# A fused retention and phase-MLP kernel: order of the DMA queue, two more transposes by DMA, and the place of the z products

## The chip, the cores and the metric

The kernel runs on one core of a Trainium2 chip. The core has TensorE (PE) for matrix products, VectorE (DVE), ScalarE (ACT) and GpSimd (POOL) for elementwise work, and SyncE (SP), which here only issues transfers to the core's 16 DMA engines. Every engine executes its own instructions in the order in which they were written, and waits at its head for what the next instruction needs; so does SyncE's queue. The metric is the device time in microseconds (us).

## The reference

The first half is a linear recurrence (retention) for 4 batches and 8 heads of 64 channels over 768 tokens; the second is an MLP that mixes tokens and channels (512 of them), with a sine and a cosine of a projection.

```python
state = gamma * state + einsum('bhd,bhe->bhde', k[:, :, t], v[:, :, t])     # per head
y[:, :, t] = scale * einsum('bhd,bhde->bhe', q[:, :, t], state)
x = y.transpose(0, 2, 1, 3).reshape(B, S, H * D)
theta = x @ w_theta
zr, zi = x * cos(theta), x * sin(theta)
u = x + w_tok_r @ zr + w_tok_i @ zi                                          # over tokens
out = u + max(u @ w_ch, 0)
```

Inputs and outputs are float32; the kernel works in bfloat16 and sums in float32.

## The kernel before

**The work and its tiles.** A *pair* is 256 tokens of one batch (all heads); there are 3 pairs per batch and 12 in all, numbered n = 0 to 11, and batch b is pairs 3b to 3b+2. An *output tile* is 128 tokens by 512 channels; there are 6 per batch and 24 in all, numbered m. Names below such as x(5) or u(5) mean the x tile of pair 5 and the u tile of output tile 5.

**Retention of a pair.** `load` (L76) brings k, q and v in float32 from DRAM, 512 KB each, into a pool of 7 buffers. `prep` (L161) casts them to bfloat16 with the decay factors (k on ScalarE, q and v on GpSimd in the later slots), in tiles named kqb. k and q are needed transposed: `flip` (L179) does that with 8 TensorE transposes into PSUM (tag "tr") and a VectorE copy out; `flip_dma` (L193) does it with one DMA transpose issued by SyncE, from SBUF to SBUF. Before the change, k goes by DMA from pair 7 on (`K_DMA`), q from pair 10 on (`Q_DMA`, L63). `ret_A` makes a block of scores (two blocks per pair, one PSUM buffer), `ret_mask` (L213) masks it on VectorE, `ret_Y` and `ret_I` make the output, transposed, from the scores and from the state, `ret_S` updates the state. `ret_out` copies the output to xT on ScalarE.

**The second half.** xT is turned into x by TensorE (`x_pe`) for pairs 0 to 4 and by a DMA transpose (`x_dma`, L288) from pair 5 on (`X_DMA`). `theta` (L309) projects xT on TensorE, and ScalarE takes the cosine and sine. `zmul` (L319) multiplies them by x on VectorE: two instructions per pair, which wait for x. `moe_M` (L327) sums the 12 products of an output tile over the batch's 6 time blocks, into one PSUM buffer (tag "y", one buffer, for most tiles). `moe_u` (L344) adds x on VectorE and so frees that buffer. `moe_U` (TensorE) or `moe_U_dma` (DMA, from slot 9 on) transposes u, `moe_O` (L365) makes the last product and `moe_out` (L372) the output tile, ot, on VectorE. `store` (L378) writes it to DRAM.

**The order.** It is written out by hand (the pools only wait for buffers). After a prologue for pairs 0 to 2, the main loop (L582) has slots n = 3 to 12. Slot n finishes pair n-1, starts pair n, prepares pair n+1, loads pair n+3, sums the output tiles `mine` (one tile in slots 3 to 6, two in slots 7 to 12), and finishes the tiles `done` of the slot before. A batch's tiles can be summed only when the z of its three pairs are there: tiles 6 and 7, of batch 1, are summed in slot 7, from z(3), z(4) and z(5), and z(5) is made in slot 6. After the loop the last tiles follow one by one.

In SyncE's queue, slot 6 holds: kT of pair 7, load of k of pair 9, x(5), loads of q and v of pair 9, the store of tile 3. In slot 7 and 8 the order is the same, one pair later; from slot 9 on there are no loads, and the transposes of u stand between. [...]

On VectorE, slots 5 and 6 (`early_z`, L670) have the two z products ahead of u of the slot's tile, slot 4 one of them; slots 7 to 12 have them after u of the first tile, ahead of u of the second and of the outputs (in slot 12 after u of its first tile, ahead of the outputs).

Of the kernel before, what the change touches and what calls it, by code (L numbers as in the profile page):

```python
# [14 lines left out]
FT = mybir.dt.float32  # L15
BF = mybir.dt.bfloat16
# [5 lines left out]
def _bcast_last(ap: bass.AP, n: int) -> bass.AP:  # L22
    return bass.AP(tensor=ap.tensor, offset=ap.offset, ap=list(ap.ap) + [[0, n]])


def _bcast_mid(ap: bass.AP, n: int) -> bass.AP:
    pat = list(ap.ap)
    return bass.AP(tensor=ap.tensor, offset=ap.offset,
                   ap=[pat[0], [0, n]] + pat[1:])
# [3 lines left out]
def kernel(  # L33
# [18 lines left out]
    B, H, S, D = q.shape  # L52
    dm = H * D
    P = 128
    HP = P // 2
    nT = S // P
# [3 lines left out]
    gammas = [1.0 - 2.0 ** (-5.0 - h) for h in range(H)]  # L60
    nG = nT // 2

    K_DMA, Q_DMA, X_DMA, U_DMA = 2 * nG + 1, 3 * nG + 1, 2 * nG - 1, 3 * nG  # L63

    ctx.enter_context(tc.manual_schedule())

# [2 lines left out]
    work = ctx.enter_context(tc.tile_pool(name="work", bufs=3))  # L69
# [6 lines left out]
    def load(n, name):  # L76

        b, g = divmod(n, nG)
        t = io.tile([P, H, 2 * D], FT, name="pair", bufs=7)
        src = dict(k=k, q=q, v=v)[name]  # L80
        nc.sync.dma_start(out=t, in_=src[b, :, 2 * g * P:2 * (g + 1) * P, :].rearrange(  # L81
            "h (p two) d -> p h (two d)", two=2))
        raw[n, name] = t
# [66 lines left out]
    for i in range(2):  # L150
        t = const.tile([P, NP, P], BF, name=f"stbd{i}")
# [9 lines left out]

    def prep(n, name, engines):
        g = n % nG
        t = work.tile([P, 2, dm], BF, name="kqb", bufs=10)
        src = raw[n, name].rearrange("p h (two d) -> p two h d", two=2)
        dst = t.rearrange("p two (h d) -> p two h d", h=H)
        if name == "k":
            if engines[0] is nc.scalar:
                nc.scalar.copy(dst, src)
            else:  # L170
                engines[0].tensor_copy(dst, src)
        else:
            sc = qscp if name == "q" else vscp
            for two in range(2):
                engines[two].tensor_mul(dst[:, two], src[:, two],  # L175
                                        _bcast_last(sc[:, 2 * g + two], D))
        st[n, name] = t
# [15 lines left out]
    def flip_dma(n, name):  # L193
        t = work.tile([P, 2, NP, P], BF, name="kqT", bufs=6)
        nc.sync.dma_start_transpose(out=t.rearrange("p w j t -> p (w j) t"),
                                    in_=st[n, name].rearrange("p w d -> p (w d)"))
        st[n, name + "T"] = t
# [40 lines left out]
    def ret_I(n, a):  # L238

        c = 2 * (n % nG) + a  # L240
        half = slice(a * HP, (a + 1) * HP)
        yT = st[n, "y"][a]
        if c > 0:
            for j in range(NP):
                nc.tensor.matmul(yT[:, j, :], stbd[c % 2][:, j, :],  # L245
                                 st[n, "qT"][:, :, j, half], start=False,
                                 stop=False, skip_group_check=True)
# [40 lines left out]
    def x_dma(n):  # L288
        b, g = divmod(n, nG)
        nc.sync.dma_start_transpose(  # L290
            out=xs[b][:, 2 * g:2 * g + 2, :].rearrange("p a (j e) -> p (a j) e", j=NP),
            in_=st[n, "xT"].rearrange("p a j t -> p (a j t)"))
# [26 lines left out]
    def zmul(n, a):  # L319
        b, g = divmod(n, nG)  # L320
        c = 2 * g + a
        nc.vector.tensor_mul(zs[b][:, c], st[n, "cs", a], _bcast_mid(xs[b][:, c, :], 2))  # L322
# [27 lines left out]
    def moe_U_dma(m):  # L350
        uT = work.tile([P, nD, P], BF, name="uT", bufs=4)
        nc.sync.dma_start_transpose(out=uT, in_=mo[m]["u"])
        mo[m]["uT"] = uT
# [17 lines left out]

    def moe_out(m):  # L372
        b, t0 = divmod(m, nT)
        ot = work.tile([P, dm], FT, name="ot", bufs=4)
        nc.vector.scalar_tensor_tensor(ot, mo[m]["o"], 0.0, mo[m]["u"], ALU.max, ALU.add)  # L375
        mo[m]["ot"] = ot

    def store(m):  # L378
        b, t0 = divmod(m, nT)
        nc.sync.dma_start(out=out[b, t0 * P:(t0 + 1) * P, :], in_=mo[m]["ot"])  # L380
# [3 lines left out]
    def w_cast(t0):  # L384
        for r in range(2):
            row = work.tile([P, S], BF, name="wrow", bufs=5)
            nc.gpsimd.tensor_copy(row, wdma[r, t0])
            wrow[r, t0] = row
# [79 lines left out]
    DP, PP = (DV, PL), (PL, PL)  # L468
# [106 lines left out]
    tiles_of = {nG - 2: [], nG - 1: [0, 1]}  # L575
    for m in range(2, nT):
        tiles_of[nG + m - 2] = [m]
    for n in range(nG + 4, B * nG + 1):
        m = nT + 2 * (n - nG - 4)
        tiles_of[n] = [m, m + 1]  # L580
    pairs = range(B * nG)
    for n in range(nG, B * nG + 1):  # L582
        mine, done = tiles_of[n], tiles_of[n - 1]
        late, two = n > nG, len(mine) > 1
        nxt = n + 1 in pairs

        if nxt and n + 1 >= K_DMA:
            flip_dma(n + 1, "k")
        if n + 3 in pairs:
            load(n + 3, "k")  # L590
        if n >= U_DMA:
            moe_U_dma(done[1])
        def preps(engines):
            prep(n + 1, "q", engines)
            prep(n + 1, "v", PP)
            if n in (nG, nG + 1):
                w_cast(n - nG + 4)

        if n == nG:
            nc.gpsimd.tensor_copy(wch, wdma["ch"])  # L600
        if nxt and n > nG + 2:
            preps(PP)
        if late:
            ret_I(n - 1, 1)

        if n in pairs:
            ret_A(n, 0)
            ret_mask(n, 0)
        if n == nG:
            moe_M(0, 5, nT)  # L610
            w_flip(1, 2)
            moe_u(0)
            moe_M(1, 4, nT)
            moe_u(1)
        if late:
            ret_Y(n - 1, 1)
            ret_S(n - 1, 1)
            ret_out(n - 1, 0, nc.scalar.copy)
            ret_out(n - 1, 1, nc.scalar.copy)
            state_out(n - 1, 1)  # L620
            if n < nG + 3:
                prep(n + 1, "k", (PL,))
                if n > nG + 1:
                    preps(DP)
            if n - 1 >= X_DMA:
                x_dma(n - 1)
        if n + 3 in pairs:
            load(n + 3, "q")

        first = mine[0]  # L630
        moe_M(first, 0, 3 if two else 2)
        if late:
            theta(n - 1, 0)
            if n - 1 < X_DMA:
                x_pe(n - 1)
            if n == nG + 1:
                preps(DP)
            theta(n - 1, 1)
        if two:
            moe_M(first, 3, nT)  # L640
            moe_u(first)
        for name, limit in (("k", K_DMA), ("q", Q_DMA)):
            if nxt and nG + 1 < n + 1 < limit and (n > nG + 1 or name == "k"):
                flip(n + 1, name)
        if n + 1 >= K_DMA and not two:
            moe_M(first, 2, 4)
        if nxt and n + 1 >= Q_DMA:
            flip_dma(n + 1, "q")
        if n + 3 in pairs:
            load(n + 3, "v")  # L650
        for t in tiles_of[n - 2]:
            store(t)
        if n + 1 >= U_DMA:
            moe_U_dma(first)

        if n in pairs:
            ret_S(n, 0)
            state_out(n, 0)
            ret_A(n, 1)
            ret_mask(n, 1)  # L660
            ret_Y(n, 0)
            ret_I(n, 0)
        if n < U_DMA:
            moe_U(done)
        if n == nG:
            prep(n + 1, "k", (AC,))
            preps(DP)
        if n == nG or n + 1 < K_DMA and not two:
            moe_M(first, 2, 4)
        early_z = late and not two  # L670
        if early_z and n > nG + 1:
            zmul(n - 1, 0)
        if n < nG + 3:
            w_tok(n - nG + 3)
        if early_z:
            zmul(n - 1, 0 if n == nG + 1 else 1)
        if not two:
            moe_M(first, 4, nT)
            if n == nG + 1:
                flip(n + 1, "q")  # L680
            moe_u(first)
            if n == nG + 1:
                zmul(n - 1, 1)
        elif n in pairs:
            moe_M(mine[1], 0, nT)
        if n + 2 in pairs and n > nG + 1:
            prep(n + 2, "k", (AC,))
        if late and not early_z:
            zmul(n - 1, 0)
            zmul(n - 1, 1)  # L690
        if two and n in pairs:
            moe_u(mine[1])
        for i, t in enumerate(done):
            if n == nG:
                flip(n + 1, "kq"[i])
            moe_O(t)
            moe_out(t)
        if n not in pairs:
            moe_M(mine[1], 0, nT)
            moe_u(mine[1])  # L700
# [43 lines left out]
```

## Time and profile before

| | |
|---|---|
| median of 14 runs | 172.72 us (169.3 to 175.29) |
| the profiled execution | 174.05 us, its span 172.3 us |
| TensorE, VectorE, ScalarE, GpSimd busy | 157.0, 102.9, 79.0, 65.3 us |
| DMA | 37.92 MB, mean 220 GB/s |
| matrix products over tokens (L340), TensorE | 97.9 us |
| DMA transposes of k or q, of x, of u | 7, 7 and 15; 4.2, 3.2 and 2.7 us from issue to landing (median) |
| loads of k, q, v of a pair | 7.1, 7.6 and 8.1 us from issue to landing (median) |

In the lines that follow, a wait is written as "engine line waited for: total us, times, longest us". In the chain and the timelines the columns are the start in us from the start of the span, the duration in us, and what ran. "SPq" is SyncE's queue, and its durations are those of the issue, not of the transfer. In the row PEclk each digit is the granted TensorE clock in one of 40 equal slices of the span, in tenths of full speed. Busy times are given with their share of the span.

### The profile page before, as it was taken

The page shows a single profiled execution, that of the slowest core. Times are in us where ns is not written, and L with a number is a line of the kernel's source. Part 1 is how long each engine was busy: PE and PEld are TensorE (multiplying, and loading weights), DVE is VectorE, ACT ScalarE, POOL GpSimd, SP SyncE. Part 2 cuts the span into 40 slices and gives each one's busy share as a digit, 9 for nine tenths or more (in the row PEclk, how much of TensorE's full clock was granted, in tenths as well). Part 3 has the DMA queues.
Part 4 walks back from the last instruction along what each step waited for, and adds up shares of the span by engine and source line. Part 5 has one row for each costly group of instructions (what it writes and reads, how often), then busy time and mean ns, then how long its engine had stood idle before and what let it go on. Part 6 is the DMA issues. An engine that isn't in the chain of part 4 may idle for free.

```text
span 172.3 us, 4660 instructions
## 1 busy us (share of the span) xinstructions
PE 157.0 (91%) x1949; PEld 88.7 (51%) x1975; DVE 102.9 (60%) x139; ACT 79.0 (46%) x137; POOL 65.3 (38%) x82
## 2 busy tenths in 40 slices
PE   7879897899999999991999999999999999999992
PEld 2345656555556766551365555554555444444461
DVE  2368896987767799435277275581855607334443
ACT  7217376643648296674283753918147170000010
POOL 5384769676688854491709045000000000000000
PEclk9999999999999999999799999999999999999999
DMA  4999999999999998999999997995817252564334
GB/s 132 306 337 319 312 325 338 254 364 305 325 305 332 290 285 252 260 215 292 233 290 238 143 314 98 250 119 108 170 31 199 47 151 62 174 142 117 91 116 160
DMA packets 66789, 37.92 MB, mean 220 GB/s; under 512 B 24144, under 2 KB 61264, under 8 KB 66768
## 3 DMA queue, kind: packets, MB, share of 16 engines
q1 hardware_dynamic: 66624, 37.50, 85.8%
q8 instruction: 15, 0.25, 0.7%
q10 hardware_dynamic: 144, 0.13, 0.2%
q14 instruction: 6, 0.05, 0.1%
HBM read 25.69 MB, written 6.29 MB: 186 GB/s over the span
## 4 chain that ended last, share of the span: by engine, by line
PE 73%; DMA 8%; SPq 7%; DVE 5%; issue 2%; ACT 2%; POOL 1%; DVEq 0%; ACTq 0%
PE y_ps L340 33%; PE o_ps L368 11%; PE th_ps L312 11%; DMA pair<-in_k_dram 5%; SPq L81 5%; PE kq_ps L183 3%; DMA x_sb<-xT 3%; PE at_ps L208 3%; PE yT_ps L231 2%; DVE z L322 2%; PE st_ps L262 2%; PE yT_ps L245 2%; PE y_ps L420 2%; DVE at L215 1%; SPq L95 1%
## 5 line engine op out<-in xcount | busy, mean ns | idle before, releaser
L340 PE MATMUL y_ps<-z,wtr 128*128 128x512 bf16 x133 | 51.2, 385 | 5.3 <-DVE u L347 3.5
L340 PE MATMUL y_ps<-z,wti 128*128 128x512 bf16 x122 | 46.7, 383 | 0.4 <-issue 0.2
L347 DVE TENSOR_TENSOR u<-y_ps,x_sb 128x512 bf16<-128x512 f32 x23 | 15.8, 689 | 28.9 <-PE y_ps L340 28.8
L215 DVE TENSOR_TENSOR at<-at_ps,maskp 128x1024 bf16<-128x1024 f32 x24 | 29.3, 1220 | 4.4 <-PE at_ps L208 4.4
L175 POOL TENSOR_TENSOR kqb<-pair,qscp 128x512 bf16<-128x512 f32 x17 | 19.2, 1140 | 27.0 <-DMA pair<-in_q_dram 25.5
L175 POOL TENSOR_TENSOR kqb<-pair,vscp 128x512 bf16<-128x512 f32 x24 | 25.6, 1085 | 6.9 <-DMA pair<-in_v_dram 6.8
L285 ACT CAST xT<-yT_ps 128x512 bf16<-128x512 f32 x20 | 13.4, 737 | 29.7 <-PE yT_ps L231 29.7
L312 PE MATMUL th_ps<-wth,xT 128*128 128x512 bf16 x93 | 23.5, 383 | 0.3
L375 DVE SCALAR_TENSOR_TENSOR ot<-o_ps,u 128x512 f32<-128x512 f32 x23 | 15.8, 690 | 12.9 <-PE o_ps L368 12.9
L368 PE MATMUL o_ps<-wch,uT 128*128 128x512 bf16 x92 | 22.8, 379 | 0.3 <-DVE ot L375 0.3
L340 PEld LDWEIGHTS <-wti 128*128 128x128 bf16 x138 | 13.6, 99 | 17.9 <-issue 4.9
L315 ACT ACTIVATE cs<-th_ps,halfpi 128x512 bf16<-128x512 f32 x24 | 16.5, 688 | 12.7 <-PE th_ps L312 12.2
L340 PEld LDWEIGHTS <-wtr 128*128 128x128 bf16 x138 | 13.6, 98 | 14.0 <-issue 0.6
L276 ACT CAST stbd<-st_ps 64x256 bf16<-64x256 f32 x40 | 14.7, 367 | 13.2 <-PE st_ps L262 12.7
L322 DVE TENSOR_TENSOR z<-cs,x_sb 128x1024 bf16<-128x1024 bf16 x24 | 18.2, 781 | 3.7 <-DMA x_sb<-xT 3.6
L316 ACT ACTIVATE cs<-th_ps,zerob 128x512 bf16<-128x512 f32 x24 | 16.5, 686 | 0.0
L312 PEld LDWEIGHTS <-xT 128*128 128x128 bf16 x96 | 9.2, 99 | 11.1 <-issue 1.0
L368 PEld LDWEIGHTS <-uT 128*128 128x128 bf16 x92 | 8.8, 98 | 10.4 <-issue 0.4
L187 DVE COPY kqT<-kq_ps 128x1024 bf16<-128x1024 bf16 x16 | 10.9, 687 | 4.7 <-PE kq_ps L183 4.4
L208 PE MATMUL at_ps<-kqT 64*64 64x128 bf16 x384 | 10.6, 221 | 2.2 <-DVE at L215 1.4
L430 ACT COPY uT<-u_ps 128x384 bf16<-128x384 bf16 (+1 forms) x2 | 0.7, 372 | 25.5 <-PE u_ps L429 25.5
L183 PEld LDWEIGHTS <-kqb 128*128 128x128 bf16 x136 | 8.8, 98 | 6.0 <-DVE kqb L175 0.9
(61 smaller groups left out, 168.4 us busy)
## 6 DMA issues: line engine op xcount, KB each, us to landing
pair<-in_k_dram SPq DMA_DIRECT2D x12, 512.0 KB, 7.1
pair<-in_q_dram SPq DMA_DIRECT2D x12, 512.0 KB, 7.6
pair<-in_v_dram SPq DMA_DIRECT2D x12, 512.0 KB, 8.1
out_dram<-ot SPq DMA_DIRECT2D x23, 256.0 KB, 2.4
wtok<-in_moe_w_tok_r_dram SPq DMA_DIRECT2D x6, 384.0 KB, 6.9
wtok<-in_moe_w_tok_i_dram SPq DMA_DIRECT2D x6, 384.0 KB, 6.4
w<-in_moe_w_theta_dram SPq DMA_DIRECT2D x1, 1024.0 KB, 8.0
w<-in_moe_w_ch_dram SPq DMA_DIRECT2D x1, 1024.0 KB, 8.8
```

What stands on the lines that cost most here:

```text
L175: engines[two].tensor_mul(dst[:, two], src[:, two], _bcast_last(sc[:, 2 * g + two], D))
L208: nc.tensor.matmul(at_ps[half, par, j, :], kT[rows, two, j, half], qT[rows, :, j, half], start=(j == 0), stop=(j == NP - 1), skip_group_ch ...
L215: nc.vector.tensor_mul(at.rearrange("p a j t -> p (a j) t"), at_ps.rearrange("p a j t -> p (a j) t"), _bcast_mid(maskp[:, two].rearrange(" ...
L276: nc.scalar.copy(stbd[(c + 1) % 2][sl, :, sl], st_ps[b][sl])
L312: nc.tensor.matmul(th_ps, st[n, "xT"][:, a, j, :], wth[:, j, :], start=(j == 0), stop=(j == NP - 1))
L315: nc.scalar.activation(cs[:, 0, :], th_ps, AF.Sin, bias=halfpi, scale=1.0)
L316: nc.scalar.activation(cs[:, 1, :], th_ps, AF.Sin, bias=zerob, scale=1.0)
L322: nc.vector.tensor_mul(zs[b][:, c], st[n, "cs", a], _bcast_mid(xs[b][:, c, :], 2))
L340: nc.tensor.matmul(y_ps, wT[r][:, s0, t0 * P:(t0 + 1) * P], zs[b][:, s0, r, :], start=(s0 == 0 and r == 0), stop=(s0 == nT - 1 and r == 1))
L347: nc.vector.tensor_add(u, mo[m]["y"], xs[b][:, t0, :])
L368: nc.tensor.matmul(o_ps, mo[m]["uT"][:, j, :], wch[:, j, :], start=(j == 0), stop=(j == nD - 1))
L375: nc.vector.scalar_tensor_tensor(ot, mo[m]["o"], 0.0, mo[m]["u"], ALU.max, ALU.add)
```

## The change

- `Q_DMA` falls from 10 to 8: q of pairs 8 and 9 is transposed by DMA as well.
- From slot 6 on, the transposes stand ahead of the loads in each slot: kT and, where it is by DMA, qT first, then x, then the loads of k, q and v. The casts of q and v of pairs 8 and later are written one slot earlier.
- From slot 6 on, the z products stand behind u and behind the outputs of the slot on VectorE.
- No output is stored in slots 6 to 8. Tiles 3 to 13, eleven stores, go out in slots 9 to 12, three, three, three and two of them.
- The pools for kqb and ot have 12 and 8 buffers (10 and 4 before).

```diff
-    K_DMA, Q_DMA, X_DMA, U_DMA = 2 * nG + 1, 3 * nG + 1, 2 * nG - 1, 3 * nG
+    K_DMA, Q_DMA, X_DMA, U_DMA = 2 * nG + 1, 3 * nG - 1, 2 * nG - 1, 3 * nG
...
-        t = work.tile([P, 2, dm], BF, name="kqb", bufs=10)
+        t = work.tile([P, 2, dm], BF, name="kqb", bufs=12)
...
-        ot = work.tile([P, dm], FT, name="ot", bufs=4)
+        ot = work.tile([P, dm], FT, name="ot", bufs=8)
...
+    def stores_in(n):
+        if n < 2 * nG:
+            return tiles_of[n - 2]
+        if n < 3 * nG:
+            return []
+        lo = 2 * nG - 3 + 3 * (n - 3 * nG)
+        return range(lo, min(lo + 3, (B - 2) * nT + 2))
...
             flip_dma(n + 1, "k")
-        if n + 3 in pairs:
+        if nxt and n + 1 >= Q_DMA:
+            flip_dma(n + 1, "q")
+        if n <= X_DMA and n + 3 in pairs:
             load(n + 3, "k")
...
-        if nxt and n > nG + 2:
+        if nG + 3 < n + 1 < Q_DMA:
             preps(PP)
...
             if n - 1 >= X_DMA:
                 x_dma(n - 1)
+        if n > X_DMA and n + 3 in pairs:
+            load(n + 3, "k")
         if n + 3 in pairs:
             load(n + 3, "q")
...
-        if nxt and n + 1 >= Q_DMA:
-            flip_dma(n + 1, "q")
         if n + 3 in pairs:
             load(n + 3, "v")
-        for t in tiles_of[n - 2]:
+        for t in stores_in(n):
             store(t)
...
-        early_z = late and not two
+        early_z = late and n < nG + 3
...
-        if late and not early_z:
-            zmul(n - 1, 0)
-            zmul(n - 1, 1)
+        if n + 2 in pairs and n + 2 >= Q_DMA:
+            prep(n + 2, "q", PP)
+            prep(n + 2, "v", PP)
         if two and n in pairs:
             moe_u(mine[1])
         for i, t in enumerate(done):
...
             moe_O(t)
             moe_out(t)
+        if late and not early_z:
+            zmul(n - 1, 0)
+            zmul(n - 1, 1)
```

## The prediction

> **What bounds the kernel now.** I read the page's busy shares first, then the waits, the chain of waits in time, and last the queues of VectorE and SyncE around the one place that these pointed to. "Slot n" is turn n of the main loop (L582), "pair n" the 256 tokens it starts on, x(n), z(n), kT(n), qT(n) that pair's tiles, and u(m), ot(m) those of output tile m.
>
> The page and its waits after 70 us:
>
> ```profile
> PE 157.0 (91%) x1949; PEld 88.7 (51%) x1975; DVE 102.9 (60%) x139; ACT 79.0 (46%) x137; POOL 65.3 (38%) x82
> ...
> PEclk9999999999999999999799999999999999999999
> ```
>
> ```profile
> DVE z L322 <- DMA x_sb<-xT: 3.6, 1, 3.6
> PE y_ps L340 <- DVE u L347: 3.5, 1, 3.5
> ```
>
> TensorE is the bound, and after 70 us it waits only once for long: 3.5 us, at 77.8. Soon after, one slice shows the only reduced clock. The chain gives the cause:
>
> ```profile
> 74.41 4.88 DMA x_sb<-xT
> ...
> 79.39 0.13 DVE z L322
> ...
> 80.68 0.61 DVE u L347
> ...
> 81.33 0.58 PE y_ps L340
> ```
>
> x(5), the first x transposed by DMA, is issued at 74.41 and lands at 79.29. VectorE has z(5) at its head, and u(5) behind it. u(5) needs nothing of x(5): its sum was done near 75.9. But the next tile's sum goes into the PSUM bank that u(5) reads (tag "y", one buffer), so TensorE stands. SyncE's queue shows why x(5) is late:
>
> ```profile
> 71.65 2.04 SPq L195 DMA_TRANSPOSE kqT<-kqb  x1
> 73.79 0.53 SPq L81 DMA_DIRECT2D pair<-in_k_dram  x1
> 74.41 1.93 SPq L290 DMA_TRANSPOSE x_sb<-xT  x1
> 76.47 0.50 SPq L81 DMA_DIRECT2D pair<-in_q_dram  x1
> 77.01 1.17 SPq L81 DMA_DIRECT2D pair<-in_v_dram  x1
> 78.70 0.40 SPq L380 DMA_DIRECT2D out_dram<-ot  x1
> 79.22 3.45 SPq L195 DMA_TRANSPOSE kqT<-kqb  x1
> ```
>
> Transfers are served in the order of issue. Spacings of landings there, from the trace's landing records: about 1.8 us for a load (k(9) 78.45 after kT(7) 76.68), 0.84 for an x transpose (79.29), 1.0 for a k transpose (85.76 after 84.73), 0.7 for a store. The queue is full until about 105 us.
>
> **The change, part by part**, in the clock of this execution: 174.05 us, that is a span of 172.3 and 1.75 around it. The median of the runs is 172.72, so this one lies 1.3 above it.
>
> *z behind the outputs.* Same instructions, other order. In slot 6 VectorE now runs u(5), ot(4), z(5), then the mask of slot 7. u(5) starts when its sum ends, 75.9, and is done at 76.6; the next sum may start at 77.8, where TensorE arrives anyway. The 3.50 us go. The clock was half from 81.03 to 84.44; TensorE worked in 3.11 us of that (from 81.33), which costs 3.11 x 1/2 = 1.56 us, and it goes with the stall. What is late next: z(5) is needed by the seventh product of tile 6, after 6 products (1.30), theta (1.73) and two products (0.43): 77.8 + 3.5 = 81.3. z takes 1.29 after x(5) has landed and ot(4) has ended (77.5), so the first half is ready at 78.2. Even with the old landing (79.29) it would be 80.0. The new wait, z on x(5), has the mask of pair 7 behind it: done at 80.0 (81.8 with the old landing), wanted by the second score block at 82.4. Covered. In slots 7 to 11 the two z (1.29) push the next slot's first mask back by that much; its reader comes about 5 us into the slot (92.8 to 98.9 in slot 8), against a mask then done by about 3.0 us. Covered by some 2 us; without that cover it would cost up to 1.3 per slot.
>
> *Transposes ahead of the loads.* x(5) passes one load: it lands at 76.68 + 0.84 = 77.5, 1.8 us earlier. The three loads of pair 9 then land at 79.3, 81.1, 82.9. The k load, now behind x(5), lands 0.9 later than before, but GpSimd and ScalarE want pair 9 only in the course of slot 7. Value on the path: nothing beyond the slack above.
>
> *q of pairs 8 and 9 by DMA.* Taken away: 2 x 8 TensorE transposes; the chain has each eight as 0.45 us, at 87.33 and 98.07, both on the path: 0.90 us. Two PSUM copies on VectorE (0.69 each) were beside the path. Added: two DMA transposes. The price of one is between 0.8 and 1.0 us of the queue (the rows above), plus its issue on SyncE, which the 7 rows of k and q transposes bound by 1.23 (idle queue) and 3.45 (full queue); I take 2.0, the usual one in the full stretch. [...] The trace has all eight blocks in 1.0 us of a full queue and a latency of 3.1 to 6.5. I take the trace: kT(8) is issued after v(9), at 78.0, and lands at 83.9; qT(8) lands at 84.9 (its input, cast by GpSimd, is ready at 75.5); x(6) lands near 85.8. Slot 8 begins, without the stall, at 92.8 - 3.50 - 1.56 - 0.45 = 87.3. Slack 2.4 us. With 3.45 us of issue for both it would land near 88.2: 0.9 us lost. For pair 9: kT and qT land by about 93, wanted at 98.6. For pairs 10 and 11 qT moves ahead of uT of the second tile and x in its slot, by one issue of 1.3 us, on a queue that waits for u and xT there anyway (102.1 to 107.9 has gaps). Its cast on GpSimd keeps its place in GpSimd's order, which is set by landings.
>
> *Loads of pairs 10 and 11* stand behind three transposes. They land at about 87.5 to 91.1 and 95.7 to 99.3, against 87.6 to 92.5 and 95.6 (last part 98.4) to 103.0 before. Slots come 5.5 to 6.0 us earlier: k(10) is wanted by ScalarE near 95.4, q(10) is needed as qT by 108. Cover of several us.
>
> *Stores held.* Three stores leave slots 6 to 8, 0.7 us each of a full queue, which pays for the two transposes. They return as three in place of two in slots 9 to 11, where the DMA share of 5 us stretches falls to between 0.3 and 1.0 and an issue is 0.4 to 0.5. Nothing waits: with eight ot buffers, tile 11 is written after store 3 has long landed. Twelve kqb buffers take no wait of note away (0.8 us on GpSimd, hidden). Zero for both; without the idle queue the stores would cost 0.7 each.
>
> **Sum:** 3.50 + 1.56 + 0.90 = 5.96; 174.05 - 5.96 = 168.1. Part of this execution's 1.3 us over the median must be the stall itself, which hangs on a landing; some is the loads before 70 us, which do not change. If none is the stall, the median becomes 172.72 - 5.96 = 166.8. I say 167.6.
>
> **The rivals.**
> *A new wait takes part of the gain.* The first score block of slot 8 waits for qT(8), by 0.9 (two slow issues) to 3 us (a load part straggles, as v(7), whose first part landed at 64.56 and the last at 68.78). For: the queue is full there. Against: 2.4 us of slack. 168.1 + 0.9 to 3 = 169 to 171, say 170. [...]
> *SyncE becomes the bound: slower.* If every transpose of slots 7 to 9 took 3.45 us to issue, slot 7 would need 3 x 3.45 + 2.2 for the loads = 12.6 us against 10.3, slot 8 12.6 against 11.4, and slot 9, with five transposes and three stores, 18.6 against 10.5. Added up, 2.3 + 1.2 + 8.1 = 11.6, less the slack of 2.4, 9.2 more, and a half clock of 1.7: 168.1 + 10.9 = 179. It outweighs the gain of 6 once the mean issue of these eleven transposes passes about 3.0 (0.45 x 11 = 5 us less than that). For: the one 3.45 lies in slot 7. Against: it was one of seven, and slots 9 and later show 1.2 to 1.9.
> *It makes no difference*, because the stall is mostly absent from the median run, and only 0.9 and small change is left: 171.5. Against: without stall and half clock this execution would be 169.0, which only the fastest run (169.3) approaches; so the median run has most of it.
>
> **How the numbers follow.** The sum as it stands 0.70 (166 to 169: the two ends of the sum, 166.8 and 168.1, with 0.8 to either side for the loads of the early slots); the partial wait 0.13 (169 to 171); no difference 0.06; SyncE bound 0.11. The range 165.8 to 171.2 holds the first two, with 0.2 at each end. About 1% (1.7 us) is what a measurement of this kernel can tell from no change. Faster by over 1%: 0.70 + 0.12 of the second, 0.82; within 1%: 0.07; slower: 0.11.
>
> **What would show it.** Right: no wait of TensorE for u of L347 after 70 us; no reduced clock there; eight transposes at L183 fewer for each of two pairs; nine rows at L195; the x transpose of slot 6 landing near 77.5; slot 8's first score block near 87. Wrong: score blocks waiting for a kqT transpose in slots 8 to 10, issues over 3 us at L195 one after another, or products at L340 waiting for z.

## The result, and the profile after

The changed kernel takes 168.64 us (median of 10 runs, 167.96 to 169.61); the kernel before, with more runs by now, 172.15 (48 runs, 169.30 to 175.67). The ratio of the two is 0.9875, with a 95% interval of 0.9845 to 0.9904. It leaves out runs that lie more than 1.5% above the fastest of their kernel, which for the kernel before are 26 of the 48; the medians contain them. So the change is faster: by 1.25% by the ratio, by 3.5 us (2.0%) by the medians. The time lies in the predicted range and 1.0 us above the predicted 167.6. The gain, forecast as 5.1 us against the median of 172.72, is 3.5 by the medians and less by the ratio; 0.6 of what is missing is the median of before itself, which more runs moved from 172.72 to 172.15.

The profiled execution took 167.97 us, its span is 166.3. Busy shares and granted clock on its page:

```profile
PE 154.6 (93%) x1933; PEld 87.1 (52%) x1959; DVE 101.2 (61%) x137; ACT 79.0 (48%) x137; POOL 66.3 (40%) x82
...
PEclk9999999999999999999999999999999999999999
```

No slice has a reduced clock. After 70 us TensorE has no wait at all in this trace. SyncE's queue in slots 6 and 7 (start, duration of the issue, what; "x2" is two in a row):

```profile
69.61 1.95 SPq L195 DMA_TRANSPOSE kqT<-kqb  x1
71.66 2.15 SPq L290 DMA_TRANSPOSE x_sb<-xT  x1
73.90 0.54 SPq L81 DMA_DIRECT2D pair<-in_k_dram  x1
...
77.04 5.78 SPq L195 DMA_TRANSPOSE kqT<-kqb  x2
82.93 1.25 SPq L290 DMA_TRANSPOSE x_sb<-xT  x1
```

and VectorE's between:

```profile
75.65 0.69 DVE L347 TENSOR_TENSOR u<-y_ps,x_sb 128x512 bf16<-128x512 f32 x1 [0.17 <-PE y_ps L340]
76.56 0.69 DVE L375 SCALAR_TENSOR_TENSOR ot<-o_ps,u 128x512 f32<-128x512 f32 x1 [0.22 <-PE o_ps L368]
77.17 1.28 DVE L322 TENSOR_TENSOR z<-cs,x_sb 128x1024 bf16<-128x1024 bf16 x2
78.37 1.22 DVE L215 TENSOR_TENSOR at<-at_ps,maskp 128x1024 bf16<-128x1024 f32 x1
```

u(5) starts as soon as its sum ends. z(5) behind it does not wait either, because x(5) landed at 75.81, and not at 79.29. The first score block of slot 8 starts at 86.97 (the prediction had 87.3, the kernel before 92.75).

Against the profile shown of before, the span is 6.0 us shorter, as the sum of 5.96 said. But that profile was one of the longer executions, and this is what the experiments turn on.

### The profile page after: what moved, and what is told of

Read it like the earlier page. It is cut to its first block, busy times and chain, and to the rows that moved or that the text cites. A ratio compares the mean times of both kernels' runs of the same rounds, so it can differ in the third digit from the quotient of the medians.

```text
span 166.3 us, 4614 instructions
## 1 busy us (share of the span) xinstructions
PE 154.6 (93%) x1933; PEld 87.1 (52%) x1959; DVE 101.2 (61%) x137; ACT 79.0 (48%) x137; POOL 66.3 (40%) x82
## 4 chain that ended last, share of the span: by engine, by line
PE 71%; DMA 15%; POOL 4%; DVE 3%; issue 2%; SPq 2%; ACT 1%; DVEq 0%; POOLq 0%
PE y_ps L340 31%; PE o_ps L368 12%; PE th_ps L312 10%; DMA pair<-in_q_dram 10%; DMA pair<-in_v_dram 6%; PE at_ps L208 3%; PE yT_ps L231 3%; PE st_ps L262 3%; PE yT_ps L245 3%; POOL kqb L175 2%; PE kq_ps L183 2%; PE y_ps L420 2%; POOL wrow L387 2%; SPq L89 1%; PE u_ps L359 1%
## 5 line engine op out<-in xcount | busy, mean ns | idle before, releaser
L340 PE MATMUL y_ps<-z,wtr 128*128 128x512 bf16 x133 | 50.5, 379 | 1.2 <-DVE z L322 0.4
L340 PE MATMUL y_ps<-z,wti 128*128 128x512 bf16 x122 | 46.2, 379 | 0.4 <-issue 0.2
L175 POOL TENSOR_TENSOR kqb<-pair,vscp 128x512 bf16<-128x512 f32 x24 | 27.1, 1150 | 4.7 <-DMA pair<-in_v_dram 4.7
L322 DVE TENSOR_TENSOR z<-cs,x_sb 128x1024 bf16<-128x1024 bf16 x24 | 17.4, 749 | 0.1
L187 DVE COPY kqT<-kq_ps 128x1024 bf16<-128x1024 bf16 x14 | 9.6, 688 | 5.1 <-PE kq_ps L183 5.0
L183 PE MATMUL kq_ps<-ident,kqb 128*128 128x128 bf16 x120 | 9.2, 219 | 1.6 <-POOL kqb L175 0.5
```

The costliest lines, as they stand in the source:

```text
L175: engines[two].tensor_mul(dst[:, two], src[:, two], _bcast_last(sc[:, 2 * g + two], D))
L340: nc.tensor.matmul(y_ps, wT[r][:, s0, t0 * P:(t0 + 1) * P], zs[b][:, s0, r, :], start=(s0 == 0 and r == 0), stop=(s0 == nT - 1 and r == 1))
```

## The experiments

Two theories. **A:** the runs of the kernel before differ by the stall ahead of slot 7 itself, which hangs on the landing of x(5), and by whether the clock halves after it. Then a gain read from one execution with a long stall and a half clock is more than most runs have to give. **B:** they differ by the loads of the first 70 us, the stall being much the same in all. The other question was which part of the change does the work.

All times in one table. "Wait" is what TensorE waited for in the main loop after 70 us in each kernel's profile. The kernel before had medians of 171.39, 173.18 and 172.07 beside the three groups E1 to E4, E5 to E8 and E9 to E12, each of which ran on another chip. Neither medians nor ratios compare well across groups: the change alone has a ratio of 0.9875 in the first measurement and of 0.9826 in E9, and ratios from 6 runs are rough. What each part does is therefore read from the profiles.

| kernel | runs | median, us | ratio to before (95%) | wait, us |
|---|---|---|---|---|
| the change | 10 | 168.64 | 0.9875 (0.9845 to 0.9904) | none |
| E1 before again | 22 | 172.04 | 1.001 (0.998 to 1.004) | 2.54 |
| E2 z alone | 14 | 169.49 | 0.9921 (0.989 to 0.9952) | none |
| E3 x ahead alone | 18 | 169.52 | 0.9917 (0.9891 to 0.9942) | none |
| E4 q by DMA alone | 6 | 173.51 | 1.0124 (1.0045 to 1.0202) | 2.25 |
| E5 the same again | 22 | 171.71 | 1.000 (0.9966 to 1.0034) | 2.21 and 0.89 |
| E6 change without z | 6 | 169.55 | 0.9811 (0.9735 to 0.9887) | 1.50, 0.48, 0.30 |
| E7 change without q | 6 | 169.17 | 0.9808 (0.9748 to 0.9867) | none |
| E8 change without hold | 6 | 170.18 | 0.9823 (0.9721 to 0.9926) | 0.53 |
| E9 the change again | 6 | 168.76 | 0.9826 (0.9775 to 0.9878) | none |
| E10 as E8 | 6 | 169.52 | 0.9823 (0.9762 to 0.9884) | 0.30, 0.33 |
| E11 x later | 6 | 175.78 | not formed | 5.20 |
| E12 more by DMA | 12 | 170.16 | 0.9903 (0.9866 to 0.994) | 1.00, 1.53 |

### E1: the kernel before, again

No edit.

> The kernel before, unchanged, to see where its runs (169.3 to 175.7 us) differ from each other. Theory A (the spread is the stall before slot 7 itself: its length hangs on the landing of x(5), and the half clock follows only when it is long): the span and the mean granted clock go together, the longest runs show a clock of 0.990 (3.41 us at half), the shortest 0.997 or more; a profile of a short run shows a wait of TensorE for u(5) of 0.5 to 2.5 us in place of 3.5 and no half clock after 70 us. Theory B (the spread comes from the loads before 70 us): the wait for u(5) stays near 3.5 us with the half clock in a short run too, and slot 6 begins 2 to 4 us earlier than at 69.2.

The profile this time is of a run of 171.44 us. The waits of TensorE after 60 us, and the clock:

```profile
PE y_ps L340 <- DVE u L347: 2.5, 1, 2.5
```

```profile
PEclk9999999999999999999999999999999999999999
```

The stall is there, but 2.54 us long, and no half clock follows. The first score block of slot 6 starts at 69.07, against 69.19 in the first profile: the first 69 us took the same time in both. The two executions differ by 2.6 us, of which 0.96 is the stall and 1.56 the half clock.

The 22 runs divide the same way. Ten have a mean granted clock of 0.99 or less, and these are the ten longest: 172.58 to 174.55, median 173.7. Twelve have 0.996 or more: 169.78 to 172.48, median 171.2. A mean of 0.99 is what one stretch of 3.41 us at half clock makes (the first profile has one, and a mean of 0.990); where it lies, only the profiled runs show. Theory A accounts for the two groups. Theory B falls for the difference between them; within each group 2 to 3 us of spread is left, and that can be the early loads (see E11).

### E2 and E3: z alone, and x ahead of the load alone

E2 takes the place of z from the change, E3 the order of x and the loads:

```diff
-        early_z = late and not two
+        early_z = late and n < nG + 3
...
-        if late and not early_z:
-            zmul(n - 1, 0)
-            zmul(n - 1, 1)
         if two and n in pairs:
             moe_u(mine[1])
...
             moe_out(t)
+        if late and not early_z:
+            zmul(n - 1, 0)
+            zmul(n - 1, 1)
```

> Of the change only the place of the z products (slot 6 on: behind u and behind the outputs). Theory A (the stall is z ahead of u on VectorE): the wait for u(5) and the half clock go although x(5) lands as late as before (near 79.3): the sum gives 174.05 - 5.06 = 169.0, and the spread of the runs shrinks from 6 us to under 2. Rival (the late landing of x(5) is the cause, whoever stands in front): a wait of 2 us or more stays, now of TensorE for z or of the score blocks for the mask, and the time stays within 1 us of before.

```diff
-        if n + 3 in pairs:
+        if n <= X_DMA and n + 3 in pairs:
             load(n + 3, "k")
...
                 x_dma(n - 1)
+        if n > X_DMA and n + 3 in pairs:
+            load(n + 3, "k")
```

> Of the change only the SyncE order: from slot 6 on the load of k stands behind the x transpose. z stays ahead of u(5). Theory A: x(5) lands 1.8 us earlier (77.5), z(5) ends at 78.8, u(5) at 79.5, so a wait of about 1.7 us is left and no half clock: 174.05 - 1.8 - 1.56 = 170.7. Rival (this part is what removes the stall): under 0.5 us left, about 169.

E2 does what was expected: 169.49 against 169.0, a spread of 1.4 us, no clock under 0.996. In its profile x(5) landed at 77.80, 8.03 us after the first score block of slot 6; by the table under E11 this would have been a stall of 1.4 us with z ahead of u. VectorE with z behind u(5) and ot(4):

```profile
76.49 0.69 DVE L347 TENSOR_TENSOR u<-y_ps,x_sb 128x512 bf16<-128x512 f32 x1 [0.17 <-PE y_ps L340]
77.41 0.69 DVE L375 SCALAR_TENSOR_TENSOR ot<-o_ps,u 128x512 f32<-128x512 f32 x1 [0.22 <-PE o_ps L368]
78.02 1.28 DVE L322 TENSOR_TENSOR z<-cs,x_sb 128x1024 bf16<-128x1024 bf16 x2
```

E3 went further than expected: 169.52, and no wait, where 1.7 us were to be left. SyncE's queue in slot 6:

```profile
69.80 2.21 SPq L195 DMA_TRANSPOSE kqT<-kqb  x1
72.10 1.57 SPq L290 DMA_TRANSPOSE x_sb<-xT  x1
73.77 0.53 SPq L81 DMA_DIRECT2D pair<-in_k_dram  x1
```

x(5) lands at 75.81, 0.78 after kT(7). In E1, with the load of k between, the two landings are 3.02 apart, so passing the load is worth 2.24 us there (1.8 in the first profile). The rest is kT(7) itself, which landed 7.49 us after the first score block of slot 6 in the profile that I reckoned from, 6.13 in E1 and 5.03 in E3, behind a load of v that landed 5.86, 4.52 and 2.97 after it. With kT(7) as late as in the first profile, about the expected 1.7 us would have been left: that E3 shows no wait at all is in part luck with the earlier loads.

From the first score block of slot 6 to that of slot 8 the profiles need 23.56 us (before), 21.09 (E1), 18.49 (E2) and 18.50 (E3). So each of the two parts can remove the whole stall by itself, and their gains do not add. One of the 18 runs of E3 still had a clock of 0.99 and took 173.67, none of the 14 of E2; that is too few to tell the two apart, but E6 below shows a stall with x ahead, and no profile with z behind u has one.

### E4 and E5: q of two pairs by DMA, alone

Beside the lines shown, the casts of q and v are written one slot earlier and kqb has 12 buffers, as in the change.

```diff
-    K_DMA, Q_DMA, X_DMA, U_DMA = 2 * nG + 1, 3 * nG + 1, 2 * nG - 1, 3 * nG
+    K_DMA, Q_DMA, X_DMA, U_DMA = 2 * nG + 1, 3 * nG - 1, 2 * nG - 1, 3 * nG
...
             flip_dma(n + 1, "k")
+        if nxt and n + 1 >= Q_DMA:
+            flip_dma(n + 1, "q")
         if n + 3 in pairs:
             load(n + 3, "k")
```

> Of the change only q of pairs 8 and 9 by DMA, issued right behind kT at the start of the slot, with the earlier casts and 12 kqb buffers. Theory A (the price of one is 1.0 us of the queue, beside the path): stall as before in slot 6, the 16 transposes less are worth 0.9 us, about 173.1 on the profiled clock, 171.3 by the median. [...]

> The kernel with only q of pairs 8 and 9 by DMA once more, since its 171.3 to 174.0 us (median 173.5) over few runs came out 2.2 above what the sum gives. Theory A (late loads before slot 4 and the half clock after the stall in slot 6, both things that vary from run to run): the runs with a clock over 0.995 lie 0.9 us under those of the kernel before (about 170.0 against 170.9), the median near 171.3, and slot 4 begins near 49.1 as elsewhere (50.4 in that profile). Rival (the part itself costs, by its two transposes in the full queue): median again 173 or more, with the loss inside slots 7 to 9.

E4 took 173.51, 2.2 above the expectation. Five of its six runs have a clock of 0.99 or less, so its ratio says little about the part itself. Its profile has loads that came late (q(4) landed at 45.78, in E1 at 44.34; slot 4 began at 50.44 in place of 49.1) and the half clock. With 22 runs (E5) the median is 171.71 and the ratio 1.000: not slower, but the 0.9 us do not appear. Runs with a clock over 0.995 have a median of 171.3, and so have those of the kernel before in the same group. E5's profile shows where it went. VectorE in slot 7, and the two products for which TensorE waited:

```profile
91.07 1.30 DVE L322 TENSOR_TENSOR z<-cs,x_sb 128x1024 bf16<-128x1024 bf16 x2 [2.93 <-DMA x_sb<-xT]
92.28 0.69 DVE L347 TENSOR_TENSOR u<-y_ps,x_sb 128x512 bf16<-128x512 f32 x1
```

```profile
81.79 0.81 PE L340 MATMUL y_ps<-z,wtr 128*128 128x512 bf16 x2 [2.21 <-DVE u L347]
...
93.02 0.81 PE L340 MATMUL y_ps<-z,wtr 128*128 128x512 bf16 x2 [0.89 <-DVE u L347]
```

qT(8) stands ahead of x(6), which lands at 90.98. z(6) is still ahead of u(7), and TensorE waits 0.89 us for u(7): the stall of slot 6 once more, one slot on. The saving on TensorE is real (below, E7), and in this profile it is spent there. Neither of my expectations had a second wait for u.

### E6, E7, E8 and E10: the change with one part undone

E6 puts z back, ahead of u and the outputs (the reverse of E2's edit):

> The whole change but with the z products where they were (ahead of u and the outputs). Theory A (either the place of z or the earlier x is enough, and both together are worth hardly more than one): near the whole change, 168.6 to 168.9, with a few runs that still wait for u(5), by 1 us or more and with a clock of 0.99. Rival (z carries the gain, x ahead alone worked by chance): a wait of 1.5 us or more in most runs, median 170 or above.

Its profile has a wait of 1.50 us for u(5), and in slots 10 and 11 two more for u, 0.48 and 0.30:

```profile
PE y_ps L340 <- DVE u L347: 2.3, 3, 1.5
```

No run of the six had a clock under 0.999, so none had a half clock behind a stall. The median, 169.55, is 0.8 to 0.9 over the change's two, but from another group, and the ratio (0.9811) is no worse than the change's: the times do not resolve it. The profile does: x ahead alone does not always suffice. Here x(5) landed 8.11 us after the first score block of slot 6, in E3 5.81, because kT(7) ahead of it landed 7.22 after it, in E3 5.03.

E7 sets Q_DMA back to 10 in the change:

```diff
-    K_DMA, Q_DMA, X_DMA, U_DMA = 2 * nG + 1, 3 * nG - 1, 2 * nG - 1, 3 * nG
+    K_DMA, Q_DMA, X_DMA, U_DMA = 2 * nG + 1, 3 * nG + 1, 2 * nG - 1, 3 * nG
```

> The whole change but with q of pairs 8 and 9 by TensorE as before. Theory A: no wait; the 16 transposes come back, 0.9 us, so 168.64 + 0.9 = 169.5. Rival (the two DMA transposes cost in the queue what they save on TensorE): within 0.3 us of 168.64.

The first score blocks of slots 7 and 9 in E7, and then in the change:

```profile
77.32 0.42 PE L208 MATMUL at_ps<-kqT 64*64 64x128 bf16 x16
...
99.89 0.42 PE L208 MATMUL at_ps<-kqT 64*64 64x128 bf16 x16
```

```profile
76.68 0.42 PE L208 MATMUL at_ps<-kqT 64*64 64x128 bf16 x16
...
98.35 0.42 PE L208 MATMUL at_ps<-kqT 64*64 64x128 bf16 x16
```

E7 needs 99.89 - 77.32 = 22.57 us for the two slots, the change 98.35 - 76.68 = 21.67, and E9 below 21.67 again. That is 0.90, as reckoned, with no wait in any of the three. The medians, 169.17 and 168.64, differ by 0.5, from different groups.

E8 and E10 store tiles 3 to 13 in the old slots:

```diff
-        for t in stores_in(n):
+        for t in tiles_of[n - 2]:
             store(t)
```

> The whole change but with the stores of tiles 3 to 13 in their old slots. Theory A (the stores were off the path): 168.64 within 0.4 us; qT(8) lands near 84.9 as before, qT(9) one store later (0.7 us). Rival (holding them is what pays for the q transposes): score blocks wait for qT in slot 8 or 9, 1 us or more.

> The whole change with the stores in their old slots once more (it gave 168.1 to 172.0 in few runs, and its profile a wait of 0.53 us for a transposed u in slot 9). If the hold was worth nothing (the prediction): the same as the whole change within 0.4 us. If it matters (a store ahead of the transposes in the full queue delays uT or qT in slots 8 and 9): 0.5 to 1.5 us above the whole change, with waits at the products with wch or the score blocks.

The medians are 170.18 and 169.52, but the ratio of E10 (0.9823) is that of the change in the same group (0.9826), and both rest on six runs. The times do not settle it. The profiles show a small price: TensorE waits 0.53 us in E8 and 0.63 in two waits in E10, both for a u transposed by DMA. In E10:

```profile
PE o_ps L368 <- DMA uT<-u: 0.6, 2, 0.3
```

The change itself has no such wait. So the hold is worth about half a microsecond in these profiles, not nothing.

### E9 and E11: the change again, and x one load later

> The whole change, unchanged, beside the kernels of this call. Theory A: 168.0 to 169.6 us, all with a clock of 0.996 or more, against a kernel before whose runs fall in two groups by the clock (about 171 and 173.5). The gain is then 2.3 us over the one group and about 5 over the other, so its median hangs on how the runs of before divide.

E9: 168.76, 167.84 to 169.83, all with a clock of 0.997 or more. The 17 runs of the kernel before beside it have five of 0.99 (172.2 to 174.5).

E11 is the kernel before with x behind the load of q as well:

```diff
-            if n - 1 >= X_DMA:
-                x_dma(n - 1)
         if n + 3 in pairs:
             load(n + 3, "q")
+        if late and n - 1 >= X_DMA:
+            x_dma(n - 1)
```

> The kernel before with one edit: x(n-1) is issued behind the load of q too, so x(5) has one more load (1.8 us) ahead of it. Theory A (stall and clock hang on the landing of x(5), one for one): x(5) lands near 80 to 81, TensorE waits 4 to 5.3 us for u(5), nearly all runs show a clock of 0.99 or less, and the median is 174.5 to 175.5. Theory B (the spread of the kernel before comes from the early loads): the median rises by 1.8 us at most and the two groups of runs stay.

The waits and the clock of its profile:

```profile
PE y_ps L340 <- DVE u L347: 5.2, 1, 5.2
```

```profile
PEclk9999999999999999998599999999999999999998
```

The median is 175.78; five of six runs have a clock of 0.99 or less. With all profiles that have z ahead of u and a stall there, the stall can be set against the time from the first score block of slot 6 to the landing of x(5):

| profile | landing less start of slot 6 | stall | difference |
|---|---|---|---|
| before | 79.29 - 69.19 = 10.10 | 3.50 | 6.60 |
| E1 | 78.22 - 69.07 = 9.15 | 2.54 | 6.61 |
| E4 | 79.35 - 70.49 = 8.86 | 2.25 | 6.61 |
| E5 | 79.75 - 70.93 = 8.82 | 2.21 | 6.61 |
| E6 | 77.65 - 69.54 = 8.11 | 1.50 | 6.61 |
| E11 | 79.52 - 68.58 = 10.94 | 5.20 | 5.74 |

The stall grows with the landing, one for one. Only E11 is off the line, by 0.87 us, which is just what its two z took longer (2.16 against 1.29). E3 is the profile with z ahead of u and no stall, and its landing, at 5.81, is under 6.61. So theory A has the cause of the stall right. In the four profiles with the old order of this queue (before, E1, E4, E5) that landing varies by 1.3 us.

Theory B has a share as well. The first score block of slot 6 starts between 68.58 (E11) and 70.93 us (E5) in the fourteen profiles, after work that is nearly the same in all. E5's profile, 173.21 us at full clock, is long mainly for that.

### E12: more of the same

```diff
-    K_DMA, Q_DMA, X_DMA, U_DMA = 2 * nG + 1, 3 * nG - 1, 2 * nG - 1, 3 * nG
+    K_DMA, Q_DMA, X_DMA, U_DMA = 2 * nG + 1, 3 * nG - 2, 2 * nG - 1, 3 * nG - 1
```

> The whole change and more of the same: q of pair 7 and u of tiles 6 and 7 by DMA too (Q_DMA 7, U_DMA 8), so 8 + 8 TensorE transposes less. If the queue still has room: 0.9 us under the whole change, 167.7. If it is full in slots 6 to 8: x(5) one transpose (1.0) later is still covered, but uT(6) and uT(7) and the loads behind them come late, and waits of TensorE for uT or of score blocks for qT take the gain back: 168.6 or more.

The median is 170.16, 1.4 above the change in the same group, although TensorE has 0.9 us less to do. The waits of TensorE after 70 us, and SyncE's queue in slots 7 and 8:

```profile
PE o_ps L368 <- DMA uT<-u: 2.5, 2, 1.5
```

```profile
78.87 6.04 SPq L195 DMA_TRANSPOSE kqT<-kqb  x2
85.02 1.24 SPq L290 DMA_TRANSPOSE x_sb<-xT  x1
...
88.94 2.45 SPq L352 DMA_TRANSPOSE uT<-u  x1
91.49 4.18 SPq L195 DMA_TRANSPOSE kqT<-kqb  x2
95.77 1.23 SPq L352 DMA_TRANSPOSE uT<-u  x1
```

uT(7) is issued at 95.77, behind two transposes that took 4.18 us to issue, and the product of tile 7 with wch waits for it 1.00 us in slot 8; tile 9's waits 1.53 in slot 9. This is the rival of the prediction in which SyncE's queue is the bound, one step beyond the change. The change of this study had the lowest median of the kernels tried.

## Why the prediction was right or wrong

**The mechanism was right**, and nearly all its places. u(5) no longer stands behind z(5), the half clock is gone, and nothing new is late. kT(8) and qT(8) landed at 83.89 and 84.86 (83.9 and 84.9 reckoned), x(6) at 86.11 (85.8). The mask behind z was never waited for. The price of one such transpose, 1.0 us of the full queue by the trace of before, held: kT(8) and qT(8) landed 0.89 and 0.97 us behind the transfers ahead of them, no score block waited for qT(8), and E7 has the 0.90 us.

**The step that failed is the one from the profiled execution to the runs.** The sum 3.50 + 1.56 + 0.90 = 5.96 was right for that execution: 174.05 - 5.96 = 168.1, and the change's profile took 167.97. But I took the stall of that run as the stall of the kernel. Two terms of the sum, 3.50 for the stall and 1.56 for the half clock, 5.06 together, were mis-sized for the other runs. In E1 the stall is 2.54 and the half clock 0, so what is to be gained there is 2.54 + 0.90 = 3.44, and E1's 171.44 less the change's 167.97 is 3.47. By the medians the gain is 3.5, which leaves 2.6 for the two terms; by the ratio it is smaller still, 1.25% or about 2.1 us, which leaves 1.2. Only two profiles of the kernel before exist, so how long the stall is in its shortest runs is not known.

The sentence "part of this execution's 1.3 us over the median must be the stall itself" named the right cause and drew half the consequence. The 166.8 that I averaged in assumed that the median run, too, has 5.06 to lose. The other end, 168.1, would have been within 0.5 of the measured time, but as a gain (4.6) still too large. Against the third rival I set the kernel's own fastest run (169.3) beside 174.05 - 5.06 = 169.0 and concluded that the median run has most of the stall. The two groups of E1, 171.2 and 173.7, show that about half of the runs lack the half clock, and E1's profile that the stall can be a quarter shorter. That rival's reason, a shorter stall in the median run, was in part right, though its time (171.5) was not.

The rival with a new wait (169 to 171) added up to 3 us of wait and no half clock, the slower one a half clock of 1.7, which is half of the 3.41 us of the first profile. No run shows a length of wait up to which no half clock comes. What the runs showed is a half clock after a wait of 2.25 us (E4), at a cost of about 1.6 us, and none after one of 2.54 (E1).

**x(5) came earlier than reckoned** (75.81, not 77.5), and by luck: it landed 0.89 us after kT(7), as reckoned (0.84), but kT(7) landed at 74.92 in place of 76.68. For the gain it made no difference, since z behind u covers either.

**The later loads were reckoned too early.** v(10) landed at 93.4 and v(11) at 104.0, not at 91.1 and 99.3. I had put 1.8 us for every load, but k, q and v of pair 10 landed 2.51, 1.81 and 2.95 us behind the transfer ahead of each, and k of pair 11 even 4.28; the profile of before, too, had v(9) 2.90 behind q(9). qT(9) came with them, at 95.16 and not 93; it was wanted at 98.35. Cover was there, but 3 us and not more. The transposes were slow to issue as well: 3.14, 2.52, 3.31, 2.78 us for the four kT and qT of slots 7 and 8, 4.31 for uT(8). The mean issue of the eleven transposes of slots 7 to 9 was 2.2, against the 3.0 from which the slower rival decides; E12 shows how near that is.

**Holding the stores is not free of effect**: zero in the sum, some 0.5 us of waits for uT when undone (E8, E10), not resolved by the times.

## What to carry to other kernels

An instruction that waits for a transfer should not stand ahead of one that frees a buffer for the bounding engine. Moving z behind cost nothing here, where its own reader comes later, and the time then hung less on when the transfer lands: the runs of E2 spread over 1.4 us, those of E1 over 4.8. Before the worth of a stall is read from one profile, compare that execution with the fastest of the kernel's runs: a stall that hangs on a landing differs from run to run (3.50 us in the first profile, 2.54 in E1), and the gain is only what the usual run has of it. Whether a half clock follows can differ as well, for nearly the same stall (2.25 us in E4 and 2.21 in E5, the same kernel; next section). Parts that cure the same wait do not add (E2 and E3), and a part that fills the transfer queue (q alone: a ratio of 1.000 in E5) can be worth nothing until another part has made the late landing harmless.

## What the runs showed of the hardware that was not expected

The half clock does not follow from the length of the stall alone. It came with a stall of 3.50 us (the first profile, from 81.03 to 84.44) and of 2.25 (E4), but not with 2.54 (E1) nor with 2.21 (E5, the same kernel as E4). The wait and the clock of E4's profile:

```profile
PE y_ps L340 <- DVE u L347: 2.3, 1, 2.3
```

```profile
PEclk9999999999999999999699999999999999999999
```

From 80 to 85 us the mean granted clock is 0.66 in E4, as much as 3.4 us at half, and 1.00 in E1. From the first score block of slot 7 to that of slot 8, E4 took 14.16 us and E5 12.55. So E4, with 2.25 us of wait, lost 1.6 more than E5 with 2.21.

In E11, with a stall of 5.20 us, the mean granted clock is 0.63 from 80 to 85 us and 0.68 from 85 to 90, together as much as 6.9 us at half. What decides, beside the stall, whether the half clock comes and how long it lasts, these runs did not show.

The two z products took 2.16 us in E11, against 1.29 in slot 6 of the first profile and 1.28 in that of the change and of E2. What made them longer in E11 no run here shows.
